# Output rows kept on chip in a ring of nine, and the third token pair loaded and turned earlier, in a retention and gated feed-forward kernel

## Chip, cores, metric

One core of a Trainium2 chip. The metric is the device time of one execution in microseconds (us), the median over several runs. All runs quoted with a ratio are fast, at a granted TensorE clock of 0.99 to 1.0 of full speed.

In the lines of the profile PE is TensorE and PEld its weight loads, DVE is VectorE, ACT ScalarE, POOL GpSimd and SP SyncE; a q behind the name stands for the engine's instruction queue.

## The reference, cut to what matters

```python
# q, k, v: (8 batches, 8 heads, 576 positions, 64);  w_gate, w_val: (512, 1536);  w_out: (1536, 512)
scores = q @ k.T / sqrt(64)                        # per batch and head
D = gamma_h ** (i - j) where i >= j, else 0        # decay, lower triangle
x = ((scores * D) @ v)  -> transposed to (4608 tokens, 512)
out = (sigmoid(x @ w_gate) * (x @ w_val)) @ w_out  # (4608, 512) float32
```

## The kernel before

It takes the tokens in two ways. The first 768 tokens are three "pairs" of 256, whose keys and queries TensorE itself transposes ("turns"). All later ones are 34 "steps" of 128 or 64 tokens: SyncE loads v, k, q; POOL scales keys and queries into `qk_nat` and spreads v into `vbd`; a transposing DMA, issued by SyncE, writes the tile `T`; TensorE takes scores, states and values from it. The feed-forward part runs over blocks of rows: gate and value products (tiles `hg`, `hv` or `h`), then output products (`op`). Pieces of the steps are put between them. The scores (`qk`) are the first to take `T`.

The first loads. Four engines issue work, but all these transfers and all stores but the last go through one queue, SyncE's, in program order:

```python
load_pair(0); load_pair(1)
load_w(0, 2); load_w(2, 2); load_w(4, 4); load_w(8, 4)   # gate and value weights
for f in range(NFC):                                    # 12 output weights
    load_wo(f)
load_pair(2)                                            # third pair: k, q, k, q, v, v
```

The steps' loads and the transpose, in the order in which SyncE gets them:

```python
def casts_to(s):
    while done["cast"] <= min(NS - 1, s):
        x = done["cast"]
        loads_to(x + (1 if x < 12 else 2))
        cast_k(x); cast_q(x)      # POOL
        cross(x)                  # SyncE: DMA transpose qk_nat -> T
        cast_v(x)                 # POOL
        done["cast"] += 1
```

Output rows: rows below 768 are held until the block at row 768 starts, later ones leave two pieces of work after their copy out of PSUM:

```python
LATE = 768
def store(opp, r0, hold, eng=None):
    ob = osb_pool.tile([P, DM], FP32, tag="osb", name=f"ob_{r0}")     # 13 buffers
    (eng or on_act)(out=ob, in_=opp)
    stores.append([hold if r0 >= LATE else 10 ** 6, r0, ob])
def tick(n=1):                    # called after every piece of work
    for x in list(stores):
        x[0] -= n
        if x[0] <= 0:
            ...                   # nc.sync.dma_start(out rows, ob)
```

The first four row tiles' output products (`op_first`) stand between the third pair's turns, scores and states, as `op_first((0,))`, turn k, `op_first((1,))`, turn q, and so on.

## Time and profile before

| | before |
|---|---|
| median of 4 runs | 341.47 us (341.12 to 341.69) |
| profiled execution | 342.36 us, span 340.7 us |
| TensorE busy | 327.6 us, 96% |
| next busiest engine | POOL, 185.2 us, 54% |

The busy share says which engine to look at; what can be won is where that engine waits. The chain that ended last (the last instruction, followed back step by step to what released it; shares of the span by engine) says the same from the other end:

```profile
PE 72%; DMA 15%; SPq 6%; POOL 3%; issue 2%; DVE 1%; ACT 1%; POOLq 0%
```

A quarter of this chain is not TensorE but transfers (DMA), SyncE's queue (SPq) and POOL. The prediction below shows the stretches, the waits and the timelines.

### The profile page before, as it was taken

Reading aid. Unit: us, or ns where it says so; the run is one execution under the profiler, and the core shown is the slowest. Engines: PE = TensorE matmul, PEld = TensorE weight load, DVE = VectorE, ACT = ScalarE, POOL = GpSimd, SP = SyncE. Lnnn points to the kernel's source line nnn. Section 1 sums busy time; section 2 is a strip of 40 time slices with the busy share of each in tenths; the row PEclk is TensorE's granted clock in tenths of the full one; section 3 lists DMA queues with packets and bytes.
Section 4 is the critical chain, followed back from the end, with each engine's and each line's share of the span. In section 5 each row is a group of like instructions: output and inputs, shape, how many; then the busy total and the mean of one; then the engine's idle time right before and its main releaser. Section 6 shows DMA issues by size and latency. Waiting matters only on the chain.

```text
span 340.7 us, 7347 instructions
## 1 busy us (share of the span) xinstructions
PE 327.6 (96%) x2749; PEld 184.2 (54%) x2784; DVE 163.2 (48%) x327; ACT 168.2 (49%) x346; POOL 185.2 (54%) x327
## 2 busy tenths in 40 slices
PE   7899989999999899899999999999999999999996
PEld 3544435969666466456556655544555555444443
DVE  5744664736466356416536625641674165603320
ACT  5645536637665356445456655444645455233321
POOL 4575569778845779598438885482657600000000
PEclk9999999999999999999999999999999999999999
DMA  7999994899999999999959999993994440020002
GB/s 202 310 352 371 354 222 96 153 216 181 205 224 261 185 184 192 245 205 255 201 146 200 181 201 227 199 181 115 198 229 99 139 64 1 2 93 33 0 31 94
DMA packets 164100, 60.00 MB, mean 176 GB/s; under 512 B 144480, under 2 KB 156000, under 8 KB 164064
## 3 DMA queue, kind: packets, MB, share of 16 engines
q1 hardware_dynamic: 163920, 59.39, 83.9%
q8 instruction: 22, 0.36, 0.5%
q14 instruction: 14, 0.11, 0.1%
q10 hardware_dynamic: 144, 0.13, 0.1%
HBM read 37.75 MB, written 9.44 MB: 139 GB/s over the span
## 4 chain that ended last, share of the span: by engine, by line
PE 72%; DMA 15%; SPq 6%; POOL 3%; issue 2%; DVE 1%; ACT 1%; POOLq 0%
PE h L490 41%; PE op L557 20%; DMA wv<-in_moe_w_val_dram 5%; DMA k<-in_k_dram 3%; PE op L733 3%; SPq L114 2%; DMA q32p<-in_q_dram 2%; SPq L105 2%; PE pv L415 2%; PE qk L394 2%; PE pv L413 2%; DMA v32p<-in_v_dram 2%; DMA wo<-in_moe_w_out_dram 2%; PE st L427 1%; POOL qk_nat L247 1%
## 5 line engine op out<-in xcount | busy, mean ns | idle before, releaser
L490 PE MATMUL h<-xT,wg_sb 128*128 128x384 bf16 (+2 forms) x476 | 102.4, 336 | 0.4 <-DVE gv L518 0.2
L490 PE MATMUL h<-xT,wv_sb 128*128 128x384 bf16 (+2 forms) x473 | 102.2, 336 | 0.4
L247 POOL TENSOR_TENSOR qk_nat<-k,ktab 64x256 bf16<-64x256 f32 x120 | 73.3, 611 | 50.0 <-PE st L427 23.4
L518 DVE TENSOR_TENSOR gv<-g,h 128x384 bf16<-128x384 bf16 (+1 forms) x96 | 59.6, 621 | 71.7 <-PE h L490 56.7
L557 PE MATMUL op<-wo_sb,gv 128*128 128x512 bf16 x356 | 84.5, 379 | 0.8
L514 ACT ACTIVATE g<-h 128x384 bf16<-128x384 f32 (+1 forms) x96 | 52.2, 544 | 64.9 <-PE h L490 58.3
L433 DVE CAST sbd<-st 64x256 bf16<-64x256 f32 x104 | 43.7, 420 | 45.1 <-PE st L427 42.9
L490 PEld LDWEIGHTS <-wg_sb 128*128 128x128 bf16 x480 | 43.7, 98 | 31.4 <-issue 0.4
L490 PEld LDWEIGHTS <-wv_sb 128*128 128x128 bf16 x480 | 44.1, 98 | 29.0 <-issue 0.4
L557 PEld LDWEIGHTS <-gv 128*128 128x128 bf16 x372 | 34.3, 98 | 36.3
L268 POOL CAST vbd<-v 64x256 bf16<-64x256 f32 x120 | 47.4, 395 | 10.7 <-PE pv L415 6.1
L528 ACT COPY ob<-op 128x512 f32<-128x512 f32 x34 | 19.8, 586 | 46.4 <-PE op L557 42.8
L278 ACT CAST vs<-v 64x256 bf16<-64x256 f32 x104 | 41.9, 403 | 1.6
L257 POOL TENSOR_TENSOR qk_nat<-q,qtab 128x512 bf16<-128x512 f32 (+1 forms) x34 | 35.4, 1041 | 2.6
L417 ACT CAST xT<-pv 128x512 bf16<-128x512 f32 (+1 forms) x34 | 18.1, 534 | 19.6 <-PE pv L415 19.5
L396 DVE TENSOR_TENSOR pt<-qk,tri 128x512 bf16<-128x512 f32 (+1 forms) x34 | 21.2, 625 | 9.0 <-PE qk L394 8.7
L415 PE MATMUL pv<-pt,vbd 128*128 128x64 bf16 x240 | 18.0, 193 | 0.0
L427 PEld LDWEIGHTS <-qk_nat 128*128 128x128 bf16 x208 | 13.2, 98 | 8.8
L413 PE MATMUL pv<-T,sbd 128*128 128x64 bf16 x216 | 17.2, 193 | 0.0
L415 PEld LDWEIGHTS <-vbd 128*128 128x128 bf16 x240 | 15.2, 98 | 3.6
L413 PEld LDWEIGHTS <-sbd 128*128 128x128 bf16 x216 | 15.1, 98 | 2.5
L394 PEld LDWEIGHTS <-T 128*128 128x128 bf16 x240 | 11.3, 98 | 8.7 <-DMA T<-qk_nat 3.5
(76 smaller groups left out, 230.3 us busy)
## 6 DMA issues: line engine op xcount, KB each, us to landing
out_dram<-ob SPq DMA_DIRECT2D x34, 256.0 KB, 2.5
v<-in_v_dram SPq DMA_DIRECT2D x26, 256.0 KB, 4.2
k<-in_k_dram SPq DMA_DIRECT2D x26, 256.0 KB, 4.7
q<-in_q_dram SPq DMA_DIRECT2D x26, 256.0 KB, 5.2
wg<-in_moe_w_gate_dram SPq DMA_DIRECT2D x12, 256.0 KB, 5.7
wv<-in_moe_w_val_dram SPq DMA_DIRECT2D x12, 256.0 KB, 5.4
wo<-in_moe_w_out_dram SPq DMA_DIRECT2D x12, 256.0 KB, 5.3
k32p<-in_k_dram SPq DMA_DIRECT2D x6, 256.0 KB, 5.5
```

Source lines behind the costliest of these rows:

```text
L247: nc.gpsimd.tensor_tensor(out=kn[half(hh), j, :, half(hh)], in0=k32[half(j), hh::2, :], in1=ktab[half(j), c, hh::2].unsqueeze(2).to_broadc ...
L257: nc.gpsimd.tensor_tensor(out=qs[0:n], in0=q32[0:n], in1=qtab[0:n, c, :].unsqueeze(2).to_broadcast([n, H, D]), op=ALU.mult)
L268: nc.gpsimd.tensor_copy(out=vb[half(hh), j, :, half(hh)], in_=v32[half(j), hh::2, :])
L278: nc.scalar.copy(out=natural["vs", s][half(hh), j], in_=loaded[s][0][half(j), hh::2, :])
L396: nc.vector.tensor_tensor(out=pt[:, :, 0:n].rearrange("p m (j t) -> p m j t", t=64), in0=qkp[:, :, 0:n].rearrange("p m (j t) -> p m j t", ...
L413: nc.tensor.matmul(pvp[:, m, half(j)], lhsT=before[:, m, :], rhs=qT[:, m, half(j)], start=True, stop=False)
L415: nc.tensor.matmul(pvp[:, m, half(j)], lhsT=vb[:, j, m, :], rhs=pt[:, m, half(j)], start=before is None, stop=True)
L433: nc.vector.tensor_copy(out=sb[half(hh), :, half(hh)], in_=st_tiles[b][half(hh)])
L490: nc.tensor.matmul(out, lhsT=w_sb[:, kc, fc * P:(fc + 1) * P], rhs=xT[:, kc, t0 + a:t0 + e], start=(kc == 0), stop=(kc == NKC - 1))
L514: nc.scalar.activation(out=g[:, 0:n], in_=h1[:, 0:n], func=AF.Sigmoid)
L518: nc.vector.tensor_tensor(out=gvs[some[0]][:, a:e], in0=g[:, 0:n], in1=h2[:, 0:n], op=ALU.mult)
L557: nc.tensor.matmul(opp, lhsT=gvs[fc][:, nb * P:(nb + 1) * P], rhs=wo_sb[:, fc, :], start=(fc == 0), stop=(fc == NFC - 1))
```

## The change

Its intent: let no store stand before a load or a transpose of the early steps, by keeping nine finished rows on chip; empty this ring over the last two blocks, when nothing is loaded any more; and take the third pair's loads ahead of most output weights, so that its turns run among the last value products instead of holding up the output products. Cut to its core:

```diff
-    for f in range(NFC):
-        load_wo(f)
-    load_pair(2)
+    pair_2 = load_pair(2)                       # now a generator, one load at a time
+    for n_wo, n_pair in ((2, 4), (6, 2), (4, 0)):
+        for _ in range(n_wo):
+            load_wo(...)
+        for _ in range(n_pair):
+            next(pair_2)
...
-    LATE = 768
+    KEEP = 9
+    def leave():
+        r, ob = stores.pop(0)
+        for p0, r0, w in rows(r, P):
+            nc.sync.dma_start(out[r0:r0 + w, :], ob[p0:p0 + w])
+    def store(opp, r0, eng=None):
         ob = osb_pool.tile([P, DM], FP32, tag="osb", name=f"ob_{r0}")
         (eng or on_act)(out=ob, in_=opp)
-        stores.append([hold if r0 >= LATE else 10 ** 6, r0, ob])
-    def tick(n=1): ...
+        stores.append((r0, ob))
+        if len(stores) > KEEP:
+            leave()
...
+    for t in vbd[0:2]:                          # moved up from behind the casts
+        nc.gpsimd.memset(t, 0.0)
     units = h_both((8, 9, 10, 11))
-    step(units, 2) ...
+    step(units, 4)                              # four gate products
+    turn("k", 2, 0, ...);  step(units, 1)       # a turn before each value product
+    turn("q", 2, 0, ...);  step(units, 1)
+    turn("k", 2, 1, ...);  step(units, 1)
+    turn("q", 2, 1, ...);  step(units, 1)
...
         for cols in ffn_units(t0, n):
-            tick()
+            pieces += 1
+            if stores and (nxt is None or w + 2 == len(BLOCKS) and pieces % 4 == 0):
+                leave()
```

The order of the output products and the third pair's scores, states and values behind that is new as well: all of `op_first((8, 9, 10, 11), range(3))` now stands directly ahead of the fourth row tile, and some casts and copies have moved to other engines.

More of the change, by code (lines that the diff above doesn't have):

```diff
@@ L117, in load_pair @@
             parts[nm, "pair", A, g] = t
+            yield
     def load_w(f, nf):
@@ L132, in load_wo @@
         parts["o", f] = t
-    load_pair(0)
-    load_pair(1)
+    for A in range(2):
+        for _ in load_pair(A):
+            pass
     load_w(0, 2)
@@ L139 @@
     load_w(8, 4)
-    for f in range(NFC):
-        load_wo(f)
-    load_pair(2)
+    pair_2 = load_pair(2)
+    for n_wo, n_pair in ((2, 4), (6, 2), (4, 0)):
+        for _ in range(n_wo):
+            load_wo(sum(1 for x in parts if x[0] == "o"))
+        for _ in range(n_pair):
+            next(pair_2)
     LEAD_CAST = 3
@@ L519, in h_units @@
                 yield 4 * n
-    LATE = 768
+    KEEP = 9
     stores = []
-    def store(opp, r0, hold, eng=None):
+    def leave():
[3 more added lines that the diff above has]
+    def store(opp, r0, eng=None):
         ob = osb_pool.tile([P, DM], FP32, tag="osb", name=f"ob_{r0}")
         (eng or on_act)(out=ob, in_=opp)
-        stores.append([hold if r0 >= LATE else 10 ** 6, r0, ob])
-    def tick(n=1):
-        for x in list(stores):
-            x[0] -= n
-            if x[0] <= 0:
-                for p0, r0, w in rows(x[1], P):
-                    nc.sync.dma_start(out[r0:r0 + w, :], x[2][p0:p0 + w])
-                stores.remove(x)
+        stores.append((r0, ob))
+        if len(stores) > KEEP:
+            leave()
     def op_units(gvs, t0, n):
@@ L560, in op_units @@
                     yield 4 * 512
-            store(opp, t0 + nb * P, 2)
+            store(opp, t0 + nb * P)
             yield 4 * 512
@@ L585, in run @@
         for _ in units:
-            tick()
+            pass
     gvs = {}
@@ L705 @@
     cast_w("v", 8, 4, 3, on_dve)
-    units = h_both((8, 9, 10, 11))
-    step(units, 2)
+    for t in vbd[0:2]:
+        nc.gpsimd.memset(t, 0.0)
     cast_wo(0, on_pool)
-    cast_wo(1, on_dve)
-    cast_wo(2, on_pool)
-    step(units, 2)
-    for f in range(3, 7):
-        cast_wo(f, on_pool if f % 2 else on_act)
-    step(units, 4)
-    for f in range(7, NFC):
-        cast_wo(f, on_pool if f % 2 else on_act)
     cast_pair("k", 2, 0, nc.gpsimd)
     cast_pair("k", 2, 1, nc.gpsimd)
+    cast_wo(1, on_dve)
+    cast_pair("q", 2, 0, nc.vector)
+    cast_pair("q", 2, 1, nc.vector)
+    units = h_both((8, 9, 10, 11))
+    step(units, 4)
+    cast_wo(2, on_pool)
+    turn("k", 2, 0, tr_psum, "tr")
+    step(units, 1)
+    cast_wo(3, on_act)
+    turn("q", 2, 0, pv_psum, "pv")
+    step(units, 1)
+    cast_wo(4, on_pool)
+    turn("k", 2, 1, tr_psum, "tr")
+    step(units, 1)
+    turn("q", 2, 1, pv_psum, "pv")
+    step(units, 1)
+    cast_wo(5, on_act)
+    cast_wo(6, on_pool)
+    cast_wo(7, on_pool)
     cast_pair("v", 2, 0, on_pool)
     cast_pair("v", 2, 1, on_pool)
-    cast_pair("q", 2, 0, nc.vector)
-    cast_pair("q", 2, 1, nc.vector)
-    nc.vector.memset(qk_nat[0], 0.0)
-    nc.vector.memset(qk_nat[1], 0.0)
-    later_constants()
-    for t in vbd[0:2]:
-        nc.gpsimd.memset(t, 0.0)
+    cast_wo(8, on_act)
+    cast_wo(9, on_pool)
+    cast_wo(10, on_act)
+    cast_wo(11, on_pool)
     loads_to(1)
@@ L736 @@
     opps = [ffn_psum.tile([P, 512], FP32, tag="ffn", name=f"op_0_{nb}") for nb in range(3)]
-    op_first((0,), range(3), opps)
-    turn("k", 2, 0, tr_psum, "tr")
-    op_first((1,), range(3), opps)
-    turn("q", 2, 0, qk_psum, "qk")
-    op_first((2,), range(3), opps)
-    turn("k", 2, 1, pv_psum, "pv")
-    turn("q", 2, 1, qk_psum, "qk")
-    op_first((3, 4), range(3), opps)
     pair_qk(2, 0, QK)
-    op_first((5, 6), range(3), opps)
+    op_first((0, 1, 2), (0,), opps)
     pair_qk(2, 1, [(tr_psum, "tr"), (pv_psum, "pv")])
-    op_first((7,), range(3), opps)
+    nc.vector.memset(qk_nat[0], 0.0)
+    nc.vector.memset(qk_nat[1], 0.0)
+    op_first((0, 1, 2), (1, 2), opps)
+    later_constants()
+    op_first((3, 4, 5), range(3), opps)
     pair_st(2, 0)
     tile_sv(2, 0, (on_act, on_act))
-    cast_dense(0, 0)
-    cast_dense(0, 1)
-    op_first((8, 9, 10, 11), range(3), opps)
+    op_first((6,), range(3), opps)
     pair_intra(2, 0, 0)
@@ L757 @@
     pair_out(2, 0, on_act)
-    store(opps[0], 0, 1, on_dve)
-    opps.append(ffn_psum.tile([P, 512], FP32, tag="ffn", name="op_0_3"))
-    op_first(range(0, 4), (3,), opps)
+    op_first((7,), range(3), opps)
     pair_intra(2, 1, 1)
@@ L763 @@
     pair_out(2, 1, on_dve)
-    store(opps[1], P, 2, on_act)
-    op_first(range(4, 8), (3,), opps)
     pair_st(2, 1)
     tile_sv(2, 1, (on_dve, on_act))
-    store(opps[2], 2 * P, 3, on_act)
-    op_first(range(8, NFC), (3,), opps)
-    store(opps[3], 3 * P, 4, on_act)
+    cast_dense(0, 0)
+    cast_dense(0, 1)
+    op_first((8, 9, 10, 11), range(3), opps)
+    store(opps[0], 0, on_dve)
+    opps.append(ffn_psum.tile([P, 512], FP32, tag="ffn", name="op_0_3"))
+    op_first(range(0, 6), (3,), opps)
+    store(opps[1], P, on_act)
+    op_first(range(6, NFC), (3,), opps)
+    store(opps[2], 2 * P, on_dve)
+    store(opps[3], 3 * P, on_act)
     for t in vbd[2:4]:
@@ L778 @@
     BLOCKS += [(t, 512) for t in range(2560, NT, 512)]
+    pieces = 0
     for w, (t0, n) in enumerate(BLOCKS):
@@ L783 @@
         begin = at
-        if t0 == LATE:
-            for i, x in enumerate(stores):
-                x[0] = 4 + 3 * i
         total = 2 * NFC * 4 * n + 12 * 512 * (n // P)
@@ L789 @@
         for cols in ffn_units(t0, n):
-            tick()
             gone += cols
+            pieces += 1
+            if stores and (nxt is None or w + 2 == len(BLOCKS) and pieces % 4 == 0):
+                leave()
             advance(begin + min(todo, -(-todo * gone // (total - 3 * 2048))))
         advance(end)
-    tick(100)
+    while stores:
+        leave()
 _INS = ['q', 'k', 'v', 'moe_w_gate', 'moe_w_val', 'moe_w_out']
```

## The prediction

> **What bounds the kernel now.** I read the page first, then the table by stretches of 10 us, then the waits of the DMA queue, then the timeline around each stretch in which TensorE does fewer matmuls than elsewhere. TensorE is the bound:
>
> ```profile
> PE 327.6 (96%) x2749; PEld 184.2 (54%) x2784; DVE 163.2 (48%) x327; ACT 168.2 (49%) x346; POOL 185.2 (54%) x327
> ```
>
> No other engine passes 54%, so only time in which TensorE waits can be won. Where is it? Columns below: stretch, length, then busy us (instructions) of PE, PEld, DVE, ACT, POOL, the clock, DMA share, GB/s.
>
> ```profile
> 40.00:50.00 10.00, 8.55 (x77) 3.64 (x76) 6.18 (x9) 3.53 (x6) 6.28 (x11) 1.00 1.04 245
> 110.00:120.00 10.00, 8.71 (x67) 4.55 (x67) 3.49 (x7) 4.70 (x12) 7.14 (x13) 1.00 1.18 179
> 140.00:150.00 10.00, 8.55 (x61) 4.20 (x61) 1.72 (x4) 2.75 (x6) 7.32 (x13) 1.00 1.21 225
> 160.00:170.00 10.00, 9.95 (x81) 5.84 (x80) 5.21 (x11) 5.02 (x11) 5.12 (x9) 1.00 1.18 199
> ```
>
> The first three rows lose 1.3 to 1.5 us of TensorE each; the last is a healthy one. Busy ends are modelled, so I also took the starts of matmuls from the trace: a 512-column one starts 216 ns after the one before it. Against such spacings, and leaving out gaps of one missing record, TensorE after 22 us loses about 3.1 us between 41.4 and 58.1, 1.35 us at 112.4, 1.51 us at 142.1 and 0.37 us at 184.0: some 6.3 us in all. Before 22 us it loses 10 us, which the change doesn't touch.
>
> The loss at 41 to 46 us is the third token pair arriving last of all first loads:
>
> ```profile
> 42.44 0.38 PE L733 MATMUL op<-wo_sb,gv 128*128 128x512 bf16 x1 [0.42 <-DVE gv L613]
> 43.28 0.40 PE L306 MATMUL kTp<-ident,kp 128*128 128x128 bf16 x4 [0.46 <-POOL kp L237]
> 43.72 0.69 DVE L237 TENSOR_TENSOR qp<-q32p,qtab 128x512 bf16<-128x512 f32 x1 [1.33 <-DMA q32p<-in_q_dram]
> 44.47 0.40 PE L306 MATMUL qTp<-ident,qp 128*128 128x128 bf16 x4
> 46.28 0.40 PE L306 MATMUL qTp<-ident,qp 128*128 128x128 bf16 x4 [0.15 <-DVE qp L237]
> ```
>
> The transposes of its keys and queries stand in TensorE's order between the first output products, so these wait for the loads too. The other two losses are waits for the transposed tile T, late because the SyncE queue was held by stores of output rows:
>
> ```profile
> SPq L536 <- ACT ob L528: 74.8, 16, 22.9
> ```
>
> (total us, times, longest), and in the timeline (start, length, what):
>
> ```profile
> 103.24 2.90 SPq L536 DMA_DIRECT2D out_dram<-ob  x5
> 106.19 0.64 SPq L105 DMA_DIRECT2D v<-in_v_dram  x1
> 106.88 0.88 SPq L105 DMA_DIRECT2D k<-in_k_dram  x1
> 109.17 3.01 SPq L284 DMA_TRANSPOSE T<-qk_nat  x1
> ...
> 113.96 0.41 PE L394 MATMUL qk<-T 128*128 128x64 bf16 x8 [1.19 <-DMA T<-qk_nat]
> ...
> 133.61 2.57 SPq L536 DMA_DIRECT2D out_dram<-ob  x4
> 139.41 2.19 SPq L284 DMA_TRANSPOSE T<-qk_nat  x1
> ```
>
> POOL had finished the input of the first transpose at 106.2 us; five stores, then the loads put ahead of it in program order, kept SyncE until 109.2. T landed at 113.92, TensorE took it at 113.96. It is the same at 139.4: input ready at 132.7, queue free only after four stores (waiting for ACT's copies) and three loads; T landed at 143.79, used at 143.84.
>
> **What the Trainium skill says.** "DMA: Bandwidth & Descriptors", section on the anatomy of one DMA: DMA engines do not wait on semaphores; the wait is made by the issuing sequencer before dispatch. The 74.8 us above agree: a store waiting for its copy holds up every load behind it. "TensorE: Matmul & The Clock Gate", section on 56 against 53.3 ns: a warm matmul costs N/2.4 GHz plus about 2.5 ns, 215.7 ns at N=512; the trace has 216. "Perfetto Trace Analysis", identifying the most-contended engine: matmul busy % is not a measure of headroom; hence the counting by starts: from 40 to 60 us the busy table leaves 1.7 us idle, the starts 3.1. The same page, on optimizing matmuls: independent groups should rotate through PSUM banks so that an evacuation overlaps the next group; the new order breaks this once, below.
>
> **Part 1: the third pair earlier.** The loads before the steps' own are DMA-bound (362 and 372 GB/s from 20 to 40 us) and their bytes don't change. Output weight 1 landed at 34.39; four pair tiles at about 0.87 us each (spacing of 44.56, 45.43, 46.33) then land at 35.3, 36.1, 37.0 and 37.9, and the output weights follow at 0.68 us each. The last one still comes at about 46.5 to 47.2. POOL scales a key tile in 1.04 us, DVE a query tile in 0.7, so all four are ready by about 38.7. The gate products end at 38.0, and the four turns now stand between value products of 0.87 us each. ACT's copies of 0.58 and 0.73 us between them keep up. I find no wait there above 0.2 us, so the value products end at 41.4 + 4 x 0.3 = 42.6.
>
> Then come 48 output products (10.37 us), scores 2 x 0.4, states 2 x 0.42, intra 0.56 + 0.3, inter 0.25: 13.1 us. Two things come on top: about 0.4 us for changing to small matmuls (from 46.73 on the kernel before needs 11.4 us for 11.0 of work), and a new wait of about 0.5 us. The fourth row tile takes the PSUM bank of the first, and nothing stands between its last product and the copy any more: copy start 0.42 after that product starts, 0.69 long, against 0.65 us of other work. End: 42.6 + 13.1 + 0.9 = 56.6, where the kernel before is at 58.1. **Gain 1.5 us**, out of 3.1.
>
> **Does T follow?** The first T landed at 59.94 and was used at 59.99, so TensorE cannot come earlier unless T does. Its POOL chain began at 52.35, after memsets of 3.7 us. Two of these memsets (1.84 us) now stand at about 33 us, where POOL was waiting for weights. With the last weight cast by 47.8, then 0.7 for the mask and 1.84 for the other two, POOL starts at about 50.4 and T comes about 2 us earlier. That is more than the 1.5 which TensorE gains, so this should hold, with only half a microsecond to spare. Steps 2, 4 and 5 had 0.06, 0.60 and 0.54 us to spare; they stand on the same POOL chain and move with it.
>
> **Part 2: the ring.** In the new order no store is issued before the transpose of step 12; before, eight were, between 90 and 106 us, each about 0.6 us of SyncE's time and 0.65 us of transfer. The loads and T of steps 8 to 13 therefore come earlier by several us: at step 9 k lands near 99 instead of 102.4 and T is issued near 103 and lands near 108, while TensorE asks at 112.4 - 1.5 = 110.9. Step 13 has two stores ahead of it instead of four, whose rows were copied long before. Both waits go: **1.35 + 1.51 = 2.86 us**. Afterwards T had 4.8 to 24 us to spare; removing waits for copies only adds to that. The 0.37 us at 184 is a queue of ACT and DVE work, which I leave. No arithmetic is added: the same 34 plus 4 store transfers, and memory traffic is the same.
>
> **Tail.** The last half row (copied at 337.37, issued at 337.77, landed at 339.55) is not moved. Its neighbour of 256 KB, issued at 336.94 before, now leaves first; worth 0.1 us at most. The rows kept over the last two blocks leave when loads have ended (the last T landed at 277.6), over queues that are nearly idle, so their drain is hidden.
>
> Sum: 1.5 + 2.86 + 0.1 = 4.5 us; 341.66 - 4.5 = **337.2 us**, 1.3% less.
>
> **Rivals.** (a) The T chain takes over: if POOL isn't free by about 51 us, because the last output weights now end the loads and their casts stand in POOL's order before the first step's, TensorE stands at steps 0 to 5 and part 1 gives 0 to 1 us. For it: slack of 0.05 us; against: the two early memsets. Time 338 to 339. (b) All 6.3 us go: the order hides the PSUM wait and the switching, and the 0.37 too; time 335.4, still under 2%. To pass 2% it would have to find more than the waits I can count. (c) Stores were not the cause, and steps 9 and 13 stay late since SyncE spends 2 to 3.5 us on each transpose and POOL 5.5 us on each step; then only part 1 counts and the time is 340. Against it: at both steps POOL's input was ready 3 and 7 us before the issue. (d) Rows kept longer run out of buffers and block ACT: thirteen buffers for nine rows and one being written; I see no such wait.
>
> **Range and chances.** From (b) and (a) with some of (c): 335.8 to 339.0. Faster by over 2% (under 334.8) needs 6.8 us, more than the countable waits: 0.05. Slower by over 2% would need a chain that stalls at every step: 0.02. Within 2%: 0.93.
>
> **What would show it.** Right: the 110 to 120 and 140 to 150 rows at about 9.95 busy, no wait of qk for T above 0.2 us there, the first h product near 56.6, SyncE's waits for ob nearly gone, a wait of about 0.5 us for the copy of the first row before the fourth tile. Wrong: a wait for T at steps 0 to 5, turns waiting for kp or qp among the value products, or a store in the tail after the last copies.

## The result, and the profile after

The changed kernel takes 337.16 us (337.05 to 337.62, 4 runs), the kernel before 341.47 us in the same rounds. The ratio is 0.9877, 95% interval 0.986 to 0.9894. A ratio here is the mean time of one kernel's fast runs over that of the other's of the same rounds, so not quite the ratio of the medians. The forecast was 337.2 us, within 2%.

The chain that ended last is now nearly all TensorE:

```profile
PE 94%; DMA 2%; DVE 1%; SPq 1%; issue 1%; ACT 0%; POOL 0%
```

The four stretches that the prediction showed (length, then busy us and instructions of PE, PEld, DVE, ACT, POOL, clock, DMA share, GB/s):

```profile
40.00:50.00 10.00, 10.00 (x136) 4.89 (x134) 5.85 (x10) 4.34 (x9) 6.84 (x13) 1.00 1.06 269
110.00:120.00 10.00, 10.00 (x78) 5.31 (x77) 3.05 (x7) 3.85 (x8) 8.32 (x15) 1.00 1.03 190
140.00:150.00 10.00, 10.00 (x83) 5.80 (x82) 2.42 (x5) 5.08 (x12) 7.69 (x16) 1.00 1.09 235
160.00:170.00 10.00, 10.00 (x74) 5.14 (x71) 2.56 (x5) 3.83 (x9) 3.85 (x7) 1.00 1.04 224
```

The three lossy rows are full. SyncE's timeline (start, length, what) shows the queue without stores up to the transpose of step 12, at 120.76 here:

```profile
101.62 2.14 SPq L289 DMA_TRANSPOSE T<-qk_nat  x1
...
120.76 3.21 SPq L289 DMA_TRANSPOSE T<-qk_nat  x1
124.02 1.05 SPq L533 DMA_DIRECT2D out_dram<-ob  x2
...
128.18 3.00 SPq L289 DMA_TRANSPOSE T<-qk_nat  x1
```

These are steps 9, 12 and 13. Step 9's transpose is issued at 101.62 us where it was 109.17, step 13's at 128.18 where it was 139.41. The tile lands 4.7 and 5.1 us before TensorE takes it, where it was 0.05 us. (0.05 us lies between landing and use wherever TensorE waits for T in these traces, so it means nothing to spare.)

At the end of the third pair stands one new wait, on TensorE's timeline; the number in brackets is idle time and what ended it:

```profile
53.16 2.75 PE L745 MATMUL op<-wo_sb,gv 128*128 128x512 bf16 x12 [0.35 <-DVE ob L538]
55.75 0.60 PE L495 MATMUL h<-xT,wg_sb 128*128 128x256 bf16 x4
...
57.61 0.40 PE L399 MATMUL qk<-T 128*128 128x64 bf16 x8
```

The fourth row tile waits for DVE to copy the first out of its bank of PSUM, the memory that TensorE writes its products to. Counted by starts it is 0.51 us (0.73 between the starts of two matmuls that are otherwise 0.216 apart). The first product of the block at row 512 starts at 55.75 (before: 58.13), and T of step 0 is taken 0.50 us after it landed.

One forecast line did not come true. SyncE's waits (total us, times, longest):

```profile
SPq L533 <- ACT ob L538: 56.3, 8, 22.9
```

They are not nearly gone. The same question asked of the kernel before from 200 us on explains it:

```profile
SPq L536 <- ACT ob L528: 69.3, 13, 22.9
```

Of its 74.8 us of waiting for copies, 69.3 stood after 200 us, where T had 11 us or more to spare, or behind the last load. Before 200 us it was 5.5 us in three waits. This waiting was never the cost.

To compare executions I use two stretches that don't depend on when the first load arrives, taken from the starts of matmuls in each trace. **A** runs from the first gate product to the first product of the block at row 512, **B** from there to the last matmul.

| profiled execution | A, us | B, us | wait at step 9 | wait at step 13 |
|---|---|---|---|---|
| before | 37.89 | 278.93 | 1.35 | 1.51 |
| changed | 36.15 | 276.06 | 0 | 0 |

A wait is the gap between the starts of two matmuls less the usual spacing. 1.74 + 2.87 = 4.61 us. The spans differ by 5.3 us because the first gate product also came 0.64 us earlier in this execution (19.60 against 20.24), where no instruction was changed. The timed difference is 4.3 us.

### The profile page after: what moved, and what is told of

Its sections match the earlier page's. It is cut to its first block, busy times and chain, and to the rows that moved or that the text cites. A ratio compares the mean times of both kernels' runs of the same rounds, so it can differ in the third digit from the quotient of the medians.

```text
span 335.4 us, 7396 instructions
## 1 busy us (share of the span) xinstructions
PE 328.0 (98%) x2784; PEld 184.3 (55%) x2784; DVE 164.2 (49%) x328; ACT 167.8 (50%) x345; POOL 185.2 (55%) x327
## 4 chain that ended last, share of the span: by engine, by line
PE 94%; DMA 2%; DVE 1%; SPq 1%; issue 1%; ACT 0%; POOL 0%
PE h L495 49%; PE op L561 24%; PE op L745 3%; PE hg L610 3%; PE hv L610 3%; PE pv L420 2%; PE qk L399 2%; PE pv L418 2%; DMA k32p<-in_k_dram 2%; PE st L432 2%; SPq L114 1%; PE op L551 1%; PE pvp L370 1%; PE idle L159 1%; PE st L345 0%
## 5 line engine op out<-in xcount | busy, mean ns | idle before, releaser
L523 DVE TENSOR_TENSOR gv<-g,h 128x384 bf16<-128x384 bf16 (+1 forms) x96 | 59.6, 621 | 71.8 <-PE h L495 56.4
L561 PE MATMUL op<-wo_sb,gv 128*128 128x512 bf16 x372 | 85.5, 379 | 0.0
L511 DVE TENSOR_TENSOR gv<-g,h 128x256 bf16<-128x256 bf16 x24 | 10.0, 420 | 13.7 <-ACT g L509 13.3
```

The costliest lines, as they stand in the source:

```text
L523: nc.vector.tensor_tensor(out=gvs[some[0]][:, a:e], in0=g[:, 0:n], in1=h2[:, 0:n], op=ALU.mult)
L561: nc.tensor.matmul(opp, lhsT=gvs[fc][:, nb * P:(nb + 1) * P], rhs=wo_sb[:, fc, :], start=(fc == 0), stop=(fc == NFC - 1))
```

## The experiments

All gave correct results. The kernel before in the rounds of each call: 341.55 us (339.64 to 342.43, 11 runs) in the first four, 341.53 us (338.98 to 343.75, 11 runs) in the next four, 341.28 us (12 runs) in the last; these 12 are the 11 before them and one new run. The first four experiments ran on one chip, all later ones on another.

### The ring alone

```diff
 (kernel before) - LATE, tick, hold   + KEEP = 9, leave, the late drain
```

> The kernel before with the ring and the late drain alone; the third pair stays behind the output weights. My theory (the two gains lie in different stretches and add): the stretch from 41 to 58 us stays as it was, both waits for T near 112 and 142 us go, 2.9 us less than before, about 338.6. Rival (the stores were not what made T late; T of steps 9 and 13 stays late because each transpose takes 2 to 3.5 us of SyncE and each step 5.5 us of POOL): 341.3, and the waits of 1.3 and 1.5 us stay in the profile.

338.46 us (338.05 to 339.16, 4 runs), ratio 0.9917 (0.9888 to 0.9945). TensorE at the two places where it had waited:

```profile
111.11 0.40 PE L394 MATMUL qk<-T 128*128 128x64 bf16 x8
...
139.47 0.28 PE L394 MATMUL qk<-T 128*128 128x64 bf16 x4
```

No bracket, so no wait. B is 276.10 us, as in the changed kernel. The rival falls: the transposes and POOL's work per step are the same, and T is in time once these stores are gone from the queue.

### The third pair alone

```diff
 (changed kernel) - KEEP, leave, the late drain   + LATE, tick, hold as before
```

> The changed kernel with the stores as in the kernel before; only the third pair's loads and turns are moved. My theory: the first h product 1.7 us earlier, and the waits at steps 9 and 13 stay at about 1.3 and 1.5 us because the whole chain of POOL and SyncE has moved earlier with TensorE: about 339.8. Rival (the chain to step 9 is held by the stores and does not move, so that TensorE, coming earlier, only waits longer there): 341.0 or more, with a wait of about 3 us at step 9.

339.77 us (339.42 to 340.39, 4 runs), ratio 0.9959 (0.9927 to 0.9991). Both waits are there again:

```profile
111.03 0.41 PE L399 MATMUL qk<-T 128*128 128x64 bf16 x8 [0.40 <-DMA T<-qk_nat]
...
140.87 0.29 PE L399 MATMUL qk<-T 128*128 128x64 bf16 x4 [1.30 <-DMA T<-qk_nat]
```

By starts they are 0.56 and 1.47 us. The chain moved with TensorE, at step 9 even by more. The two ratios multiply to 0.9876, against 0.9877 for the whole change: the parts add, as far as intervals of 0.3% to either side can show.

### The two POOL memsets put back

```diff
-    for t in vbd[0:2]:
-        nc.gpsimd.memset(t, 0.0)
     ... 
     later_constants()
+    for t in vbd[0:2]:
+        nc.gpsimd.memset(t, 0.0)
```

> The changed kernel with the two POOL memsets (1.84 us) put back behind the casts of the output weights, where the kernel before had them. My theory (T of step 0 is the limit of part 1, with 0.50 us to spare): T of step 0 lands 1.8 us later, TensorE waits 1.3 us there, and part 1 is nearly lost: about 338.5. Rival (POOL's start does not matter, k and q of step 0 come from the queue at about that time anyway, or the wait is made up later): 337.2 to 337.4, no wait at step 0.

339.09 us (338.66 to 339.57, 4 runs), ratio 0.9933 (0.9906 to 0.9961); more than expected.

```profile
59.71 0.41 PE L399 MATMUL qk<-T 128*128 128x64 bf16 x8 [1.84 <-DMA T<-qk_nat]
...
67.11 0.41 PE L399 MATMUL qk<-T 128*128 128x64 bf16 x8 [0.18 <-DMA T<-qk_nat]
```

By starts, 2.00 us at step 0 and 0.34 at step 1. POOL began the first step at 52.06 us instead of 49.53: 1.84 us of memsets, and 0.7 because this execution's last output weights landed later. The ring alone took 338.46 us: with 1.84 us of zeroing in the wrong place, part 1 gains nothing.

### The first row tile's products first

```diff
-    op_first((8, 9, 10, 11), range(3), opps)
+    op_first((8, 9, 10, 11), (0,), opps)
+    op_first((8, 9, 10, 11), (1, 2), opps)
     store(opps[0], 0, on_dve)
```

> The changed kernel with the last four products of the first row tile ahead of those of the other two, so that its copy out of PSUM runs beside eight products and the fourth tile does not wait for it. My theory: the wait of 0.52 us goes, T of step 0 (0.50 us to spare) just holds and that of step 2 (0.26) costs a little: 0.3 to 0.5 us less than the changed kernel, 336.7 to 336.9. Rival (the T chain takes all of it): a wait of 0.1 to 0.3 us at each of steps 0 and 2 and no change, 337.2.

336.74 us (336.57 to 337.48, 6 runs), ratio 0.9869 (0.9846 to 0.9891). The twenty products around the change of bank run without a gap, and T of step 0 (57th us) has nothing to spare; TensorE waits 0.03 us for it:

```profile
50.76 4.48 PE L745 MATMUL op<-wo_sb,gv 128*128 128x512 bf16 x20
55.08 0.60 PE L495 MATMUL h<-xT,wg_sb 128*128 128x256 bf16 x4
...
56.97 0.41 PE L399 MATMUL qk<-T 128*128 128x64 bf16 x8
```

A is 35.64 us, 0.51 less. But 0.4 us needs a run beside the changed kernel on one chip.

### The changed kernel again, and the same beside it

> The changed kernel once more, unaltered, as the yardstick of this chip for the three beside it: 337.2, 1.2% less than the kernel before.

337.49 us (337.18 to 338.13, 6 runs), ratio 0.9886 (0.9853 to 0.992).

> The kernel with the first row tile's products first, once more, beside the changed kernel on the same chip. My theory (the wait of 0.52 us for the PSUM copy was on the path, and T of step 0 just holds): 0.3 to 0.5 us less than the changed kernel. If the 0.4 us seen before was chance: no difference.

337.57 us (336.78 to 338.08, 6 runs), ratio 0.9884 (0.9849 to 0.9918). In the profile the gain is there again (A 35.64, B 276.06), in the time it is not: two of six executions took 336.8, four 337.3 to 338.1. With nothing to spare at step 0 in the first profile and 0.05 us more in this one, an execution in which T lands later loses what the bank change gained. That this happens in the slower ones is an inference from the profiled executions: over the five of the changed kernel, or of kernels equal to it up to there, T of step 0 landed at 57.08 to 58.33 us and TensorE waited 0, 0, 0, 0.18 and 0.42 us for it.

### A ring of three

```diff
-    KEEP = 9
+    KEEP = 3
```

> The changed kernel with a ring of three rows in place of nine. No store waits for a copy then either (a row leaves when the third one after it has been written), but seven stores fall between 70 and 117 us, among the loads and transposes of steps 4 to 10. Theory A (what the ring removes is the time that stores take from SyncE and the transfer queue in the tight stretch): T of step 4, with 0.94 us to spare, comes 1.2 to 1.9 us later, waits of 0.3 to 1 us appear at steps 4 or 5, and the time is 337.7 to 338.2. Theory B (what the ring removes is the waiting of the queue for copies not yet made): no new wait, 337.2.

338.20 us (337.52 to 338.59, 4 runs), ratio 0.9902 (0.9861 to 0.9944). SyncE's and TensorE's timelines:

```profile
74.68 1.44 SPq L289 DMA_TRANSPOSE T<-qk_nat  x1
76.21 1.69 SPq L533 DMA_DIRECT2D out_dram<-ob  x2
77.96 0.46 SPq L105 DMA_DIRECT2D v<-in_v_dram  x1
...
80.67 2.96 SPq L289 DMA_TRANSPOSE T<-qk_nat  x1
```

```profile
85.96 0.41 PE L399 MATMUL qk<-T 128*128 128x64 bf16 x8 [0.46 <-DMA T<-qk_nat]
```

Two stores whose rows were copied long before, and which therefore wait for nothing, take 1.7 us of the queue; step 5's tile is late and TensorE waits 0.63 us. (In this execution it also waited 0.42 us at step 0. One store stands ahead of that transpose; it was out at 53.84 us, and POOL's input came at 54.51. The ring-only runs start with as little to spare there and don't wait at step 5.) B is 277.12, which is 276.06 + 0.42 + 0.63. The queue theory ("A") holds in the profile: what the ring takes away is the stores' room in the queue, not their waiting. The times alone don't show it, since the runs overlap (the changed kernel beside it: 337.18 to 338.13).

Two things in this trace go beyond that. Against the first ring-only profile, T of step 5 was issued 0.37 us later but landed 1.71 us later: most of the delay came after the transpose had started, and not from waiting its turn. And two stores stand between the transposes of steps 8 and 9, three between those of 12 and 13, yet T had 3.0 and 3.3 us to spare there: a few stores are harmless where the chain is not late already.

### No early drain

```diff
-            if stores and (nxt is None or w + 2 == len(BLOCKS) and pieces % 4 == 0):
-                leave()
```

> The changed kernel without the early leaving in the last two blocks, so that nine rows leave only after the last copy. My theory (a store of 256 KB takes about 0.65 us of transfer and the drain hides nine of them): 5.5 us more than the changed kernel, about 342.7, more than the kernel before. If the transfers overlap better than that: 339 to 341.

343.33 us (343.22 to 343.75, 4 runs), ratio 1.0059 (1.001 to 1.0108): 5.8 us more than the changed kernel in the same rounds.

```profile
331.90 5.58 SPq L533 DMA_DIRECT2D out_dram<-ob  x9
```

Nine stores at 0.62 us each, from about the start of the last matmul on, moving 371 to 383 GB/s with nothing beside them. A ring without its drain is slower than no ring.

### The kernel before, twice more, and the ring alone once more

The waits above are from one profile of the kernel before, and its times scatter far more (338.98 to 343.75) than those of the changed one (337.18 to 338.13). No edit; one execution each, state unknown.

> The kernel before, unaltered, profiled a second time. In the first profile TensorE needed 37.89 us from the first gate product to the first product of the block at row 512, but the ring-only run, which is the same program up to there, needed 36.55 with the third pair's tiles landing evenly. Theory: this stretch varies with when these tiles land, 36.5 to 38.0 us; from there to the last matmul it is 278.9 us as in the first profile, within 0.3. Rival: the first profile was typical, 37.9 again.

> The same a third time, to see the spread: as the run before.

> The ring alone a second time. The stretch up to the first product of the block at row 512 anywhere from 36.5 to 38.0 us, as for the kernel before; from there to the last matmul 276.1 us as in the first run of it and in the changed kernel. If that second part moved by more than 0.3 us, the 2.8 us of the ring would not be a fixed sum.

They took 338.40, 339.02 and 338.35 us.

| profiled execution | A, us | B, us | wait at step 9 | wait at step 13 |
|---|---|---|---|---|
| before, second | 36.88 | 276.47 | 0.34 | 0 |
| before, third | 36.68 | 276.86 | 0.30 | 0.29 |
| third pair alone | 36.15 | 278.12 | 0.56 | 1.47 |
| ring alone | 36.55 | 276.10 | 0 | 0 |
| ring alone, second | 37.24 | 276.23 | 0 | 0 |
| changed, second | 36.16 | 276.05 | 0 | 0 |
| first row first, both runs | 35.64 | 276.10, 276.06 | 0 | 0 |

My expectation that B stays at 278.9 fell. The second profile of the kernel before, TensorE at step 9:

```profile
111.51 0.41 PE L394 MATMUL qk<-T 128*128 128x64 bf16 x8 [0.17 <-DMA T<-qk_nat]
```

There the tile landed 0.05 us before its use again, but TensorE had waited 0.34 us and not 1.35. So the two waits are not a fixed sum. They are what is left of a chain with nothing to spare, from 0 to 1.5 us per place; and the old order costs between 36.55 and 37.89 us in A. Both of these executions are at the fast end: the timed runs of the kernel before are around 341.3. With the ring of nine B is 276.05 to 276.27 in eight of nine profiles (the ninth is the one with the memsets late), and with the new order A is 36.15 or 36.16 in all six without the bank change.

### The last two memsets on DVE

```diff
 (first row tile's products first)
     nc.vector.memset(qk_nat[1], 0.0)
+    for t in vbd[2:4]:
+        nc.vector.memset(t, 0.0)
...
-    for t in vbd[2:4]:
-        nc.gpsimd.memset(t, 0.0)
```

> The kernel with the first row tile's products first, and with the remaining two memsets (1.84 us of POOL) given to DVE, which is idle from 46.7 to 49.8 us. POOL can then begin the first step when its keys land (48.4 to 49.6 us) instead of 0.9 to 1.2 us later, so that T of step 0 has about 1 us to spare in place of 0.04 to 0.10. My theory (T of step 0, which lands up to 1.2 us later in some runs, eats the 0.5 us in those): 0.5 us less than the changed kernel, 336.7 to 337.0, in all runs. Rival (the spread between runs comes from the loads before 40 us, not from T): same as the changed kernel, 337.3.

336.93 us (336.41 to 337.09, 6 runs), ratio 0.9865 (0.9829 to 0.9901). POOL's timeline:

```profile
47.28 0.52 POOL L208 TENSOR_SCALAR_AFFINE_SELECT tri<-tri 64x64 bf16<-64x64 bf16 x2
48.77 2.64 POOL L252 TENSOR_TENSOR qk_nat<-k,ktab 64x256 bf16<-64x256 f32 x4 [0.97 <-DMA k<-in_k_dram]
```

POOL now waits for the keys instead of zeroing, and T of step 0 has 1.02 us to spare. The slowest of six runs is faster than the fastest of the changed kernel on the same chip (337.18), and the spread is 0.7 us. It was run at another time. With that reservation it is the fastest version on this chip, by about 0.6 us over the changed kernel's 337.49. (The first row tile's products alone took 336.74 on the other chip and 337.57 on this one.) The rival (the spread comes from the loads before 40 us) fits less well, since those are unchanged and the spread of the same kernel without this edit was 1.3 us; six runs of each don't exclude it.

## Why the prediction was right, and where it was not

- **TensorE is the bound, and only its waits can be won.** Right: between 20 us and the end two waits of more than 0.2 us are left, 0.51 us for the PSUM copy and the 0.37 us that the prediction left out (now at 178.8), and the chain is 94% TensorE.
- **Part 1, 1.5 us.** The profile gave 1.74, with the first h product at 55.75 (56.4 if the first gate product had come as late as before; forecast 56.6). The timed part alone is 0.41% of 341.5, 1.4 us. But I took a single execution for the rule: against the others of the old order it is 0.4 to 1.1 us, because how long TensorE waits there depends on when single tiles land. In the first profile one query tile landed 1.6 us after the key tile before it; the ring alone, with the same program up to there, had 0.85. Part 1 bundles the load order, the turns' places, the memsets and the order of the output products; only the memsets and the bank order were tested apart.
- **The new wait of 0.5 us for the PSUM copy.** Right, 0.51; the run that removes it shows A shorter by 0.51.
- **T of step 0 follows with half a microsecond to spare.** Right: 0.50. The memsets on POOL were the lever, as putting them back shows. What I missed is that this half microsecond varies between executions of the new order, from 0.73 us to spare down to waits of 0.18 and 0.42.
- **Part 2, 2.86 us.** The size is right in the first pair of profiles (B shorter by 2.87) and in the time (0.83% of 341.5, 2.8 us). T of step 9 was issued at 101.62 and landed at 105.51, earlier than forecast (103 and 108). Again it is a typical value, not a fixed one: 0.4 and 0.8 us against the two later profiles of the kernel before. That the forecast of the sum came out to the tenth is therefore partly luck: it rests on one execution (342.36 us).
- **The step that failed: "four stores (waiting for ACT's copies)", and the 74.8 us as proof of it.** At 133.6 us SyncE did not wait: the transpose of step 12 ended at 133.5, the stores began at 133.6. Up to 200 us the stores waited 5.5 us, at neither of the two places. What held the queue was the time to issue them and the transfers put in ahead of T, as the ring of three shows; how much of it is SyncE's time and how much the DMA engines', no run settles. The forecast survived this because the ring removes both the stores' room and their waiting.
- **"SyncE's waits for ob nearly gone".** Wrong for the same reason; 56.3 us of harmless waiting remain.
- **Tail, 0.1 us at most.** From the start of the last matmul to the end of the span it was 3.60 us and is 3.57.
- **Rivals.** (c) falls by the ring alone, (a) did not happen but was near (the memsets late produce it), (d) shows once and costs nothing: near 226 us ACT waits 2.1 us for a store to give its buffer back, and TensorE has no gap there. (b) would have needed 6.3 us; the first-row version and the memsets on DVE recover part of the difference.

What stays open: why the waits at steps 9 and 13 vary so much between executions of the kernel before. Single landings that come 0.7 us later or more in a stream of loads are seen in several traces, but no run here settles what makes them late, nor that they explain the times of 343. Open too: whether SyncE's time or the DMA engines' was short. In both kernels the DMA share is 1.01 to 1.45 in every stretch of 10 us from 70 to 170 us, so the DMA engines were never idle for long there.

## What to carry to other kernels

A queue that carries loads and stores in one order is a chain of its own: count how much a tile has to spare when it is used, step by step, because with nothing to spare one store more or a memset on a helper engine becomes a wait, and how long it is changes from run to run. The total of a wait list says little: ask where it stands, and what comes behind it. A gain that rests on one profile of a kernel with no slack should be checked against a second profile of the same kernel.

## What the Trainium skill lacked or had wrong

- "TensorE: Matmul & The Clock Gate", section on the back-to-back issue gap, gives about 131 ns per matmul at N=512 for a stream of weight loads and matmuls, and says that N/2.4 + 2.5 counts too much there. Here such a stream (each 512-column matmul with its own weight load) has starts 216 ns apart, 384 columns 162 to 163 ns, 256 columns 109 ns: the formula holds, the 131 ns do not.
- "DMA: Bandwidth & Descriptors", section on the anatomy of one DMA, puts the sequencer's dispatch at about 50 ns and calls descriptor generation small and variable, for the GpSimd path. For other engines the page says that the sequencer's time to start a DMA is usually small beside the DMA itself, and its part on trn3 has 512 sequencer cycles per copy for "previous generations"; how this time grows in a loaded SyncE queue on trn2 stands nowhere. Here issuing a 256 KB store kept SyncE 0.33 us on an idle queue and 0.4 to 1.7 us under load, a load up to 3.4 us, a transposing DMA 1.2 to 4.8 us. Part of this may be the transfers backing up: the nine stores of the run without a drain, with nothing beside them, kept SyncE 0.38 to 0.41 us each for the first four and 0.54 to 0.61 us for the last five.
